# A new opening for an attention and mixture-of-experts kernel: loads in head order, three banks for the running sum, first passes before the bias rows

## The chip, the cores and the metric

The kernel runs on one core of a Trainium2 chip. The metric is the device time of one execution in microseconds (us); lower is better. TensorE (PE) multiplies, ACT (ScalarE), DVE (VectorE) and POOL (GpSimd) do the element-wise work, and SP (SyncE) issues most of the DMAs. PEld is TensorE's loading of weights, which overlaps its matmuls.

## The reference

Attention with a bias that forgets, then a routed layer of experts. There are 8 batches, 8 heads, 576 positions and a head size of 64.

```
scores = q @ k.T / sqrt(64)                       # per batch and head
cum    = cumsum(maximum(s, 0), axis=-1)
scores = where(causal, -1e9, scores + minimum(-(cum[:, None] - cum[None, :]), 0))
attn   = softmax(scores)
x      = attn @ v                                 # to (8 * 576, 512)
logits = x @ w_gate + modality_bias[modality_id]  # 8 experts
e      = argmax(logits); gate = softmax(logits)[e]
out    = gate * (relu(x @ w1[e]) @ w2[e])
```

## The kernel before

The class `Attn` works on 32 pairs, each of two batches (`ab` = 0, 1) of one head. A pair has nine chunks of scores in the order `ORDER = (3, 7, 2, 6, 8, 1, 5, 0, 4)`: chunks 0 to 3 are four blocks of 128 queries of the first batch, 4 to 7 those of the second, and chunk 8 is the last 64 queries of both. A chunk's scores come from two passes of TensorE into one PSUM bank. The first pass (L307, L321 for chunk 8) multiplies QH by KA, that is, the high half of q by the high half of k on partitions 0 to 127, with the low half of k on the lower partitions. The second (L308, L322) multiplies QL by KB: 64 partitions hold the low half of q and the high half of k, and 12 more hold the bias. Of these, ten rows of QL are constant ones and zeros (`rows`), ten rows of KB are taken from `ek`, and two rows of QL are the queries' own sums (`eq`) against rows of -1 in KB. `ek` holds the running sum less its value at the start of each block, in a high half (lower 64 partitions) and a low half (upper 64).

DVE evicts a chunk with the causal mask `mk` and the row's extreme (L310, L324), ACT takes the exponential (L330), TensorE transposes it (L340), ACT or DVE copies it into PT (L343, L359), and TensorE multiplies by V (L380) and by `pw` and `pq` (L274), which hold the identity and the gate's weights. There are four banks for scores (`sp`, SPB = 4). From one pair to the next GpSimd prepares QH, QL and KA (`prep`: L250 makes high halves, L254 low halves), and SP places rows of `ek` and `eq` (`place`: L207, L209). Loads of q, k and v stand in `load_qk` and `load_v` (L232, L237), with two buffers for q and k and three for v.

The order of the instructions on each engine is fixed ahead of the run by a scheduler that goes by program order and readiness; `issue_after` puts an instruction behind another one on the same engine. Each engine takes its instructions in that order and waits at the one whose inputs are missing.

The opening is the constructor. It loads s (576 columns, 128 partitions), pairs 0 and 1 of q, k and v, and the gate's weights (`setup`). ACT scales s by 8 (L84); DVE forms the running sum with three scans into two banks (L92); ACT copies its upper half (L99) and makes `ek`'s parts (L108); DVE makes the low half (L109). ACT also makes the unit of `pq` (L141), QL's constant rows of both buffers (L180, L181), `eq` (L119, L121), and pair 0's part of KB (L192). GpSimd makes masks (L167 to L174) and pair 0's QH and KA (L196 to L198), DVE pair 0's QL (L193). `prep(1)` on GpSimd and the hook `R.consts` at step 7 (L514 to L536) follow during pair 0.

Of the kernel before, what the change touches and what calls it, by code (L numbers as in the profile page):

```python
# [7 lines left out]
F32 = mybir.dt.float32  # L8
F32R = mybir.dt.float32r
# [22 lines left out]

class Attn:
# [3 lines left out]
    def __init__(self, ctx, tc, qkv, s, ident, wg):  # L37
# [9 lines left out]
        self.xo = self.ps2.tile([P, 512], F32, name="ox")  # L47
        self.QH = [c.tile([P, 2, 640], F32R, name=f"QH{u}") for u in range(2)]
        self.QL = [c.tile([P, 2, 640], F32R, name=f"QL{u}") for u in range(2)]
# [22 lines left out]
        eq = self.eq = t1.tile([P, KW], F32R, name="eq")  # L72
# [6 lines left out]
        nc.vector.memset(self.pw, 0.0)  # L79
        self.unit(self.pq, 0)  # L80
        self.setup(wg)
        s8 = t1.tile([P, KW], F32, name="s8")
        for k in (slice(0, 256), slice(256, KW)):
            i = nc.scalar.activation(s8[:, k], sr[:, k], AF.Relu, scale=8.0)  # L84
        with self.tc.issue_after(i.ins):
            self.rows(ho, 0)
        cum = [self.ps1.tile([P, 512], F32, name="sp", bufs=SPB) for _ in range(2)]
        last = 0.0
        for c, k in ((cum[0], slice(0, 256)), (cum[0], slice(256, 512)), (cum[1], slice(0, 64))):
            w = k.stop - k.start  # L90
            at = 512 if c is cum[1] else k.start
            nc.vector.tensor_tensor_scan(c[:, k], s8[:, at:at + w], zz.broadcast_to([P, w]), last, ALU.add, ALU.add)  # L92
            last = c[:, k.stop - 1:k.stop]
        nb = t1.tile([P, 5], F32, name="nb")
        nc.vector.tensor_scalar(nb[:, :4], cum[0][:, 0:512:P], -1.0, None, ALU.mult)
        nc.vector.tensor_scalar(nb[:, 4:], cum[1][:, :1], -1.0, None, ALU.mult)
        cl = self.ps1.tile([P, 512], F32, name="pt")
        with self.tc.issue_after(self.act):
            i = nc.scalar.copy(cl[up], cum[0][up])  # L99
        self.act = i.ins  # L100
        ekf = ek.bitcast(F32)
        for c in (3, 2, 1, 4, 0):
            n = min(P * (c + 1), KW)
            with self.tc.issue_after(self.act):
                for g in range(2 if c == 4 else 1):
                    k = slice(512 * g, min(n, 512 * g + 512))
                    w = k.stop - k.start
                    i = nc.scalar.activation(ek[:, c, k], cum[g][:, :w], AF.Identity, bias=nb[:, c:c + 1])  # L108
                    lo = nc.vector.scalar_tensor_tensor(ek[up, c, k], (cum[1] if g else cl)[up, :w], nb[up, c:c + 1], ekf[up, c, k], ALU.add, ALU.subtract)  # L109
            self.act = i.ins  # L110
        self.prep0(raw, 0)

        dg = ekf.rearrange("p c k -> p (c k)")
        up = slice(64, P)

        def own(u, ab):
            with self.tc.issue_after(self.act):
                r = slice(64 * u + 32 * ab, 64 * u + 32 * ab + 32)
                nc.scalar.copy(eq[r, 64 * ab:64 * ab + 512].rearrange("p (c q) -> p c q", c=4),  # L119
                               dg[r, :2816].rearrange("p (c x) -> p c x", c=4)[:, :, :P])  # L120
                self.act = nc.scalar.copy(eq[r, 512 * (1 - ab):512 * (1 - ab) + 64], dg[r, 2816:]).ins  # L121

        own(0, 0)
        own(0, 1)
        self.hold[0] = lo.ins
        for ab in range(2):
            own(1, ab)
            with self.tc.issue_after(self.act), self.tc.issue_after(self.hold[0]):
                self.prep0(raw, 1 + ab)
        self.place(0)  # L130
        with self.tc.issue_after(self.act):
            self.rows(ho, 1)
        with self.tc.issue_after(self.act):
            self.unit(self.pw, XW)
        self.place(1)

    def unit(self, t, w):

        for ab in range(2):
            rows = slice(64 * ab, 64 * ab + 64)  # L140
            self.act = self.nc.scalar.copy(t[rows, :, w * ab:w * ab + 64], self.ident[rows, 64 * ab:64 * ab + 64].unsqueeze(1).broadcast_to([64, 8, 64])).ins  # L141

    def save(self, u):
# [7 lines left out]
        nc.sync.dma_start(self.eqd[:, u], self.eq.bitcast(F32)[r])  # L151

    def hot(self, t1):
# [14 lines left out]
        nc.gpsimd.affine_select(out=self.mk[:, 384:512], in_=self.mk[:, 384:512], pattern=[[-1, P]],  # L168
                                compare_op=ALU.is_ge, fill=NEG, base=0, channel_multiplier=1)
        nc.gpsimd.memset(self.KB[1].bitcast(F32)[64:96], -1.0)  # L170
        for ab in range(2):
            rows = slice(64 * ab, 64 * ab + 64)
            nc.gpsimd.affine_select(out=self.mk[rows, 736:], in_=self.mk[rows, 736:], pattern=[[-1, 64]],
                                    compare_op=ALU.is_ge, fill=NEG, base=0, channel_multiplier=1)  # L174
        return ho

    def rows(self, ho, u):
        nc = self.nc
        for a, (m, l) in enumerate(((0, 512), (64, 0))):
            nc.scalar.copy(self.QL[u][64:96, a, m:m + 512].rearrange("p (c q) -> p c q", c=4), ho[64:96, :4].unsqueeze(2).broadcast_to([32, 4, P]))  # L180
            self.act = nc.scalar.copy(self.QL[u][64:96, a, l:l + 64], ho[64:96, 4:5].broadcast_to([32, 64])).ins  # L181

    def prep0(self, raw, part):
# [6 lines left out]
        if part:  # L190
            for a in (part - 1,):
                self.act = nc.scalar.copy(KB[lo, a], rk[lo, a]).ins  # L192
                self.hold[0] = nc.vector.tensor_tensor(QL[lo, a, :KW], rq[lo, a], QHf[lo, a, :KW], ALU.subtract).ins  # L193
            return
        for a in range(2):
            nc.gpsimd.tensor_scalar(QH[:, a, :KW], rq[:, a], 1.0, 1.0, ALU.mult, ALU.mult)  # L196
            nc.gpsimd.tensor_scalar(KA[:, a], rk[:, a], 1.0, 1.0, ALU.mult, ALU.mult)
            self.last = nc.gpsimd.tensor_tensor(KA[lo, a], rk[lo, a], KAf[lo, a], ALU.subtract).ins  # L198

    def place(self, pi):  # L200
# [3 lines left out]
        if pi < 8:  # L204
            for u, ab in ((0, 0), (0, 1), (1, 0), (1, 1)):
                r = 32 * ab + pi
                nc.sync.dma_start(KB[64 + 5 * u:69 + 5 * u, ab], self.ek.bitcast(F32)[64 * u + r:64 * u + r + 1])  # L207
                if u:
                    self.sp = nc.sync.dma_start(QL[74:76, ab, :KW], self.eq.bitcast(F32).rearrange("(u p) k -> u p k", u=2)[:, r]).ins  # L209
# [1077 lines left out]
```

## Time and profile before

| what | value |
|---|---|
| median of three runs | 848.71 us (848.46 to 849.37) |
| the profiled execution | 848.76 us |
| its span in the profile | 847.0 us, 16786 instructions |
| TensorE busy | 809.5 us, 96% of the span |
| weight loads | 702.4 us, 83% |
| DVE, ACT, GpSimd busy | 554.7, 537.7 and 359.3 us (65%, 63%, 42%) |
| DMA | 182.01 MB, mean 215 GB/s |

The span is the time from the first to the last recorded work of the execution; its own time has a little around it. Busy shares are means over stages with different limits. All times below are microseconds from the start of the span.

### The profile page before, as it was taken

What the parts mean: (1) busy time and instruction counts of PE and PEld (TensorE: products, weight loads), DVE (VectorE), ACT (ScalarE), POOL (GpSimd) and SP (SyncE); (2) the same over time, 40 slices, a digit from 0 to 9 for tenths busy, and PEclk for the clock granted to TensorE, in tenths of its full rate; (3) what the DMA queues carried; (4) which work ended last, traced back from release to release, by engine and by line L of the source; (5) the groups of instructions that cost most, each with busy time, mean ns of one, the idle gap of its engine ahead of it and who ended that gap; (6) DMA issues with size and microseconds to landing.
All of it is one profiled execution on the core that took longest, in us unless ns stands there. A gap on an engine that the chain in (4) does not pass through costs nothing. (4 is left out here: it accounts for less than half of the span.)

```text
span 847.0 us, 16786 instructions
## 1 busy us (share of the span) xinstructions
PE 809.5 (96%) x5636; PEld 702.4 (83%) x5636; DVE 554.7 (65%) x1516; ACT 537.7 (63%) x1287; POOL 359.3 (42%) x379
## 2 busy tenths in 40 slices
PE   3999999999999999999999999999999999999993
PEld 2888888888888887887888999998888899999872
DVE  6666667666766667666579876555666666565772
ACT  7888888788888888876365454444445555454561
POOL 9668767888679876992400010000000000000000
PEclk9999999999999999999999999999999999999997
DMA  5675555776557655547598776655555666655950
GB/s 180 191 219 176 176 176 177 225 226 205 167 154 233 194 176 175 188 159 280 187 382 303 287 273 252 223 206 209 207 200 216 249 252 252 250 224 208 336 196 7
DMA packets 69336, 182.01 MB, mean 215 GB/s; under 512 B 9727, under 2 KB 9727, under 8 KB 69120
## 3 DMA queue, kind: packets, MB, share of 16 engines
q1 hardware_dynamic: 63408, 160.86, 56.1%
q0 software_dynamic: 5840, 20.06, 6.1%
q8 instruction: 45, 0.74, 0.3%
q14 instruction: 43, 0.35, 0.1%
HBM read 144.76 MB, written 26.80 MB: 203 GB/s over the span
## 5 line engine op out<-in xcount | busy, mean ns | idle before, releaser
L977 POOL DMA_INDIRECT out<-ys,oi x36 | 36.2, 1006 | 369.7 <-DVE ys L976 262.6
L310 DVE CUSTOM_DVE_ANT_0 pe<-sp,mk 128x512 f32<-128x512 f32 (+3 forms) x256 | 120.6, 488 | 57.2 <-PE sp L308 53.3
L330 ACT ACTIVATE pe<-pe,mx 128x512 f32<-128x512 f32 (+3 forms) x256 | 145.1, 567 | 14.1 <-DVE mx L310 8.3
L993 ACT ACTIVATE hT<-hp 128x512 fp32r<-128x512 f32 x72 | 42.8, 596 | 166.6 <-PE hp L991 147.9
L343 ACT COPY PT<-pt 128x512 f32<-128x512 f32 (+3 forms) x256 | 107.3, 419 | 31.3 <-PE pt L340 27.4
L340 PE MATMUL pt<-ident,pe 128*128 128x128 f32 x640 | 120.3, 283 | 0.4 <-ACT PT L343 0.2
L380 PE MATMUL o<-PT,V 128*64 128x320 f32 (+4 forms) x896 | 106.9, 364 | 6.1 <-DVE PT L359 6.1
L307 PE MATMUL sp<-KA,QH 128*128 128x256 f32 (+2 forms) x256 | 99.8, 399 | 11.7 <-POOL KA L198 11.5
L380 PEld LDWEIGHTS o<-PT,V 128*64 128x64 f32 x896 | 70.2, 136 | 43.0 <-DVE PT L359 13.0
L991 PE MATMUL hp<-xT,wcb 128*128 128x256 f32 x648 | 89.7, 282 | 1.1 <-DVE hT L994 1.1
L340 PEld LDWEIGHTS pt<-ident,pe 128*128 128x128 f32 x640 | 76.0, 144 | 16.7 <-ACT PT L343 7.4
L308 PE MATMUL sp<-KB,QL 76*128 76x256 f32 (+2 forms) x256 | 87.0, 342 | 2.6 <-DMA QL<-eq 2.5
L991 PE MATMUL hp<-xT,wca 128*128 128x256 f32 x624 | 87.3, 282 | 0.7 <-ACT xT L947 0.5
L254 POOL TENSOR_TENSOR KA<-rawk,KA 64x576 fp32r<-64x576 f32 x62 | 87.0, 1422 | 0.2
L254 POOL TENSOR_TENSOR QL<-rawq,QH 64x576 fp32r<-64x576 f32 x62 | 86.5, 1412 | 0.1
L994 DVE SCALAR_TENSOR_TENSOR hT<-hp,hT 128x512 fp32r<-128x512 f32 x72 | 49.5, 688 | 55.4 <-ACT hT L993 55.4
L991 PEld LDWEIGHTS hp<-xT,wcb 128*128 128x128 f32 x648 | 83.1, 188 | 2.0 <-DVE hT L994 1.3
L991 PEld LDWEIGHTS hp<-xT,wca 128*128 128x128 f32 x624 | 80.4, 188 | 1.8 <-issue 1.0
L970 PE MATMUL y<-wcb,hT 128*128 128x512 f32 x336 | 81.2, 398 | 0.0
L970 PEld LDWEIGHTS y<-wcb,hT 128*128 128x128 f32 x336 | 62.7, 188 | 14.6
L250 POOL TENSOR_SCALAR KA<-rawk 128x576 fp32r<-128x576 f32 x62 | 41.9, 688 | 65.5 <-PE sp L307 47.7
L991 PE MATMUL hp<-xT,wcc 128*128 128x256 f32 x456 | 64.7, 281 | 0.5 <-DVE hT L994 0.5
(280 smaller groups left out, 1627.4 us busy)
## 6 DMA issues: line engine op xcount, KB each, us to landing
wrbw<-in_w SPq DMA_DIRECT2D x104, 512.0 KB
wraw<-in_w SPq DMA_DIRECT2D x56, 512.0 KB
rawq<-in_qkv SPq DMA_DIRECT2D x32, 576.0 KB
rawk<-in_qkv SPq DMA_DIRECT2D x32, 576.0 KB
xg<-lists SPq DMA_DIRECT2D x18, 576.0 KB
V<-in_qkv SPq DMA_DIRECT2D x32, 320.0 KB
KB<-KA SPq DMA_DIRECT2D x62, 144.0 KB
lists<-z SPq DMA_DIRECT2D x8, 576.0 KB
```

Of the source, the lines that this page charges most:

```text
L254: self.last = nc.gpsimd.tensor_tensor(o, i, h, ALU.subtract).ins
L307: self.pe.append(nc.tensor.matmul(sp[:, :nn], QH[:, q0:q0 + P], KA[:, ab, :nn], start=True, stop=False).ins)
L308: self.pe.append(nc.tensor.matmul(sp[:, :nn], QL[:EXT, q0:q0 + P], KB[:EXT, ab, :nn], start=False, stop=True).ins)
L310: ins = nc.vector.tensor_tensor_reduce(out=t[:, :n], in0=sp[:, :n], in1=self.mk[:, 512 - n:512], scale=-0.125, scalar=3.0e38, op0=ALU.add, ...
L330: self.act = nc.scalar.activation(t[:, :n], t[:, :n], AF.Exp, bias=m, scale=-1.0, accum_out=st["sums"][:, o:o + 1]).ins
L340: self.pe.append(nc.tensor.transpose(out=pt[:, P * j:P * j + P], in_=pe[:, P * j:P * j + P], identity=self.ident).ins)
L343: cp(w[:, :, v:v + P], pt[:, :P * (c + 1)].rearrange("p (j q) -> p j q", q=P))
L380: m = nc.tensor.matmul(o[r, f - q0:q1 - q0], V[:, ab, j, :], PT[ab][:, PTS * j + f if j < 4 else PTW - 64:PTS * j + q1 if j < 4 else PTW], ...
L970: self.last[0] = nc.tensor.matmul(y[u], hT[:, a, f, P * u:P * u + P], W[4 + f // 2][:, c, 512 * (f % 2):512 * (f % 2) + 512], start=f == 0 ...
L991: nc.tensor.matmul(hp[:, u], W[k][:, a, f:f + P], xT[:, c, k], start=k == 0 and i == 0, stop=k == 3 and i == 2)
L993: hi = nc.scalar.activation(hs, hp, AF.Relu)
L994: lo = nc.vector.scalar_tensor_tensor(hT[:, 1, 2 * m:2 * m + 2], hp, 0.0, hs.bitcast(F32), ALU.max, ALU.subtract)
```

## The change

- **Loads.** s comes in two halves, pair 0's q and k in four loads, one batch at a time, and pair 1's k ahead of its q. V[1] and pair 2's q and k are issued at the end of the constructor, behind pair 1's rows, in place of pair 2's load at step 7 of pair 0.
- **Running sum.** Three banks of 256, 256 and 64 columns; the last value goes through a small SBUF tile; `ek` is made in pieces of at most 256 columns.
- **Bias rows.** `eq` is gone: its two rows go from `ek` into QL by DMA (`place_q`, two for the blocks and two for the last 64 queries). KB's ten rows of one batch go in one DMA (`place_k`), the first of them issued by ACT. `save` copies own rows out of `ek` in four DMAs. QL's constant rows are made once, half by ACT and half by GpSimd, and copied to the second buffer by DMA; QL lies in a longer tile.
- **Pair 0 and pair 1.** The part of KB that holds k comes by DMA from KA in place of ACT copies. Pair 1's high halves are made by ACT (`prep1`) in place of GpSimd; its low halves stay in `prep`.
- **GpSimd.** The masks go behind pair 0's KA; the units of `pw` and `pq` are made by GpSimd at step 6. `R.consts` goes to step 14.
- **TensorE.** Forty transposes of the identity into a scratch bank at the start, and the first passes of chunks 3, 7, 2 and 6 of pair 0 ahead of any second pass, with four such transposes behind each. The second passes of pair 0 keep the order of the chunks until the first product with V.

```diff
-        self.xo = self.ps2.tile([P, 512], F32, name="ox")
+        self.QLx = [c.tile([P, 1408], F32R, name=f"QL{u}") for u in range(2)]
...
-        nc.sync.dma_start(sr, s)
-        raw = self.load_qk(0)
-        self.raw[1] = self.load_qk(1)
-        for pi in range(2):
-            self.V[pi] = self.load_v(pi)
+        for k in HALVES:
+            nc.sync.dma_start(sr[:, k], s[:, k])
+        raw = self.raws()
+        for a in range(2):
+            for u in range(2):
+                nc.sync.dma_start(raw[u][:, a], self.qkv[0, :, KW * (2 * u + a):KW * (2 * u + a + 1)])
+        nc.vector.memset(self.pw, 0.0)
+        self.raw[1] = self.load_qk(1, (1, 0))
+        self.setup(wg)
+        self.V[0] = self.load_v(0)
...
+        self.warm(WARM)
+        self.rows(ho)
...
+        cum = [self.ps1.tile([P, 512], F32, name="sp", bufs=SPB) for _ in range(3)]
+        for g, w in enumerate((256, 256, 64)):
+            nc.vector.tensor_tensor_scan(cum[g][:, :w], s8[:, 256 * g:256 * g + w], zz.broadcast_to([P, w]), last, ALU.add, ALU.add)
+            n = (w + P - 1) // P
+            nc.vector.tensor_scalar(nb[:, 2 * g:2 * g + n], cum[g][:, 0:w:P], -1.0, None, ALU.mult)
+            if g < 2:
+                last = end[:, g:g + 1]
+                nc.vector.tensor_copy(last, cum[g][:, w - 1:w])
+                with self.tc.issue_after(self.act):
+                    self.act = nc.scalar.copy(cl[up, 256 * g:256 * g + w], cum[g][up, :w]).ins
...
+        self.place_k(0, 0)
+        self.sp = nc.sync.dma_start(self.QL[1].bitcast(F32)[64:74, :, :KW], self.QL[0].bitcast(F32)[64:74, :, :KW]).ins
+        self.place(0)
+        for ab in range(2):
+            with self.tc.issue_after(self.hold[0]):
+                self.prep0(raw, 1 + ab)
+        with self.tc.issue_after(self.act):
+            self.prep1()
+        with self.tc.issue_after(self.last):
+            self.masks()
+        with self.tc.issue_after(self.sp):
+            self.sp = nc.sync.dma_start(self.KB[1].bitcast(F32)[:64], self.KA[1].bitcast(F32)[64:]).ins
+        with self.tc.issue_after(self.sp):
+            self.place(1)
+        with self.tc.issue_after(self.sp):
+            self.raw[2] = self.load_qk(2)
+        with self.tc.issue_after(self.sp):
+            self.V[1] = self.load_v(1)
+        self.more = {6: self.units}
...
+    def prep1(self):
+        rq, rk = self.raw[1]
+        for t, r in ((self.KA[1], rk), (self.QH[1], rq)):
+            for a in range(2):
+                self.act = nc.scalar.copy(t[:, a, :KW], r[:, a]).ins
...
+            self.last = self.nc.gpsimd.tensor_copy(t[rows, :, w * ab:w * ab + 64], self.ident[rows, 64 * ab:64 * ab + 64].unsqueeze(1).broadcast_to([64, 8, 64])).ins
...
         for a in range(2):
             nc.gpsimd.tensor_scalar(QH[:, a, :KW], rq[:, a], 1.0, 1.0, ALU.mult, ALU.mult)
             nc.gpsimd.tensor_scalar(KA[:, a], rk[:, a], 1.0, 1.0, ALU.mult, ALU.mult)
+            nc.sync.dma_start(KB.bitcast(F32)[lo, a], KAf[up, a])
...
+    def warm(self, n):
+        for _ in range(n):
+            i = self.nc.tensor.transpose(out=self.xo[:, :P], in_=self.ident, identity=self.ident).ins
+        return i
...
+            if st["pi"] == 0 and not st["s"]:
+                for j in ORDER[:SPB]:
+                    self.high(st, j)
+                    with self.tc.issue_after(self.pe[-1]):
+                        self.pe.append(self.warm(WARM2))
+            sp = st["high"][i] if i in st["high"] else self.high(st, i)
...
-                with self.behind():
+                with self.behind() if pi or not self.pe else self.tc.issue_after(self.pe[-1]):
...
-                if k % 9 == 7 and pi + 2 < npair:
+                if k % 9 == 7 and 0 < pi < npair - 2:
...
-            setup = {5: A.consts, 7: R.consts, 17: lambda: A.save(0), 26: lambda: A.save(1), 20: lambda: R.setup(mid, mb, A.t1p)}
+            setup = {**A.more, 5: A.consts, 14: R.consts, 17: lambda: A.save(0), 26: lambda: A.save(1), 20: lambda: R.setup(mid, mb, A.t1p)}
```

## Rows read from the trace of the kernel before

**Rows 1.** Windows: busy of PE, PEld, DVE, ACT, POOL; granted clock; DMA share; GB/s.

```profile
0.00:20.00 20.00, 5.55 (x14) 3.66 (x15) 12.54 (x31) 15.73 (x35) 18.03 (x29) 1.00 0.58 190
20.00:847.00 827.00, 804.00 (x5623) 698.78 (x5622) 542.18 (x1488) 521.99 (x1253) 341.28 (x351) 0.99 0.63 215
...
5.00:10.00 5.00, 0.00 (x0) 0.00 (x0) 3.13 (x8) 4.99 (x14) 3.87 (x6) 1.00 1.00 378
```

**Rows 2.** Waits, 0 to 25 us: waiter and releaser, total, times, longest.

```profile
PE sp L307 <- POOL KA L198: 11.5, 2, 10.2
...
PE sp L308 <- DMA QL<-eq: 2.5, 1, 2.5
```

**Rows 3.** Timeline of ACT and DVE: start, length, engine, line, work, idle before.

```profile
3.59 0.78 ACT L84 ACTIVATE s<-sr 128x256 f32<-128x256 f32 x2 [1.53 <-DMA sr<-in_s]
...
4.04 0.70 DVE L92 TENSOR_TENSOR_SCAN sp<-s,zz 128x256 f32<-128x256 f32 x1 [0.20 <-ACT s L84]
...
6.73 0.57 ACT L99 COPY pt<-sp 64x512 f32<-64x512 f32 x1
...
8.04 2.37 DVE L109 SCALAR_TENSOR_TENSOR ek<-pt,nb,ek 64x512 fp32r<-64x512 f32 x4 [1.83 <-ACT ek L108]
...
10.51 0.38 DVE L109 SCALAR_TENSOR_TENSOR ek<-pt,nb,ek 64x128 fp32r<-64x128 f32 x1
...
10.92 3.08 DVE L193 TENSOR_TENSOR QL<-rawq,QH 64x576 fp32r<-64x576 f32 x2
```

**Rows 4.** Timeline of SP's DMA issues: start, length of the issue.

```profile
9.73 2.03 SPq L237 DMA_DIRECT2D V<-in_qkv  x1
...
11.88 2.40 SPq L207 DMA_DIRECT2D KB<-ek  x3
...
14.38 0.57 SPq L209 DMA_DIRECT2D QL<-eq  x1
```

**Rows 5.** Timeline of TensorE, pair 0 and the start of pair 1.

```profile
16.21 1.08 PE L308 MATMUL sp<-KB,QL 76*128 76x512 f32 x2 [2.47 <-DMA QL<-eq]
...
17.77 0.61 PE L321 MATMUL sp<-KA,QH 128*128 128x288 f32 x1 [0.47 <-DVE mx L310]
...
18.92 1.05 PE L340 MATMUL pt<-ident,pe 128*128 128x128 f32 x4
...
20.25 0.44 PE L322 MATMUL sp<-KB,QL 76*128 76x288 f32 x1
...
20.49 0.44 PE L321 MATMUL sp<-KA,QH 128*128 128x288 f32 x1
...
21.41 0.60 PE L340 MATMUL pt<-ident,pe 128*128 128x128 f32 x4
...
23.07 0.47 PE L307 MATMUL sp<-KA,QH 128*128 128x512 f32 x1
...
28.88 0.65 PE L274 MATMUL ox<-pw,oT 128*128 128x144 f32 x4
```

**Rows 6.** Timeline of DVE's evictions and ACT's exponential of chunk 8.

```profile
17.01 0.69 DVE L310 CUSTOM_DVE_ANT_0 pe<-sp,mk 128x512 f32<-128x512 f32 x1 [3.02 <-PE sp L308]
...
18.84 0.69 DVE L310 CUSTOM_DVE_ANT_0 pe<-sp,mk 128x512 f32<-128x512 f32 x1 [1.13 <-PE sp L308]
...
22.18 0.78 ACT L330 ACTIVATE pep<-pep,mx 128x576 f32<-128x576 f32 x1
```

**Rows 7.** Timeline of GpSimd, and last its low halves by line (ns, least, median, most).

```profile
4.77 0.86 POOL L173 TENSOR_SCALAR_AFFINE_SELECT mk<-mk 64x64 f32<-64x64 f32 x2
...
5.72 0.75 POOL L196 TENSOR_SCALAR QH<-rawq 128x576 fp32r<-128x576 f32 x1
...
7.47 0.67 POOL L197 TENSOR_SCALAR KA<-rawk 128x576 fp32r<-128x576 f32 x1 [1.00 <-DMA rawk<-in_qkv]
...
12.22 2.31 POOL L250 TENSOR_SCALAR KA<-rawk 128x576 fp32r<-128x576 f32 x2
...
L254 POOL TENSOR_TENSOR KA<-rawk,KA x62: 1400/1420/1447, 18.5 to 366.6; 64x576 fp32r<-64x576 f32 x62
```

More of the change, by code (lines that the diff above doesn't have):

```diff
@@ L30 @@
 QUIET = (1, 5, 6)
+HALVES = slice(0, 256), slice(256, KW)
+WARM = 40
+WARM2 = 4
 class Attn:
@@ L78, in __init__ @@
             nc.vector.memset(ek.bitcast(F32)[:, c, P * (c + 1):], 0.0)
-        nc.vector.memset(self.pw, 0.0)
-        self.unit(self.pq, 0)
-        self.setup(wg)
+        self.xo = self.ps2.tile([P, 512], F32, name="ox")
+        self.warm(WARM)
+        self.rows(ho)
         s8 = t1.tile([P, KW], F32, name="s8")
[L83 to L96, printed above, removed]
-        cl = self.ps1.tile([P, 512], F32, name="pt")
-        with self.tc.issue_after(self.act):
-            i = nc.scalar.copy(cl[up], cum[0][up])
-        self.act = i.ins
+        for k in HALVES:
+            with self.tc.issue_after(self.act):
+                self.act = nc.scalar.activation(s8[:, k], sr[:, k], AF.Relu, scale=8.0).ins
+        cum = [self.ps1.tile([P, 512], F32, name="sp", bufs=SPB) for _ in range(3)]
+        cl = self.ps1.tile([P, 512], F32, name="pt")
+        nb, last = t1.tile([P, 5], F32, name="nb"), 0.0
+        end = t1.tile([P, 2], F32, name="end")
+        for g, w in enumerate((256, 256, 64)):
[7 more added lines that the diff above has]
+                    self.act = nc.scalar.copy(cl[up, 256 * g:256 * g + w], cum[g][up, :w]).ins
         ekf = ek.bitcast(F32)
@@ L103, in __init__ @@
             n = min(P * (c + 1), KW)
-            with self.tc.issue_after(self.act):
-                for g in range(2 if c == 4 else 1):
-                    k = slice(512 * g, min(n, 512 * g + 512))
+            for g in range((n + 255) // 256):
+                k = slice(256 * g, min(n, 256 * g + 256))
+                with self.tc.issue_after(self.act):
+                    self.act = nc.scalar.activation(ek[:, c, k], cum[g][:, :k.stop - k.start], AF.Identity, bias=nb[:, c:c + 1]).ins
+            for t, k in ((cl, slice(0, min(n, 512))), (cum[2], slice(512, n))):
+                if k.start < k.stop:
@@ new lines, in __init__, with masks @@
+        self.more = {6: self.units}
+    def masks(self):
+        nc = self.nc
+        nc.gpsimd.affine_select(out=self.mk[:, 384:512], in_=self.mk[:, 384:512], pattern=[[-1, P]],
+                                compare_op=ALU.is_ge, fill=NEG, base=0, channel_multiplier=1)
+        for ab in range(2):
+            rows = slice(64 * ab, 64 * ab + 64)
+            nc.gpsimd.affine_select(out=self.mk[rows, 736:], in_=self.mk[rows, 736:], pattern=[[-1, 64]],
+                                    compare_op=ALU.is_ge, fill=NEG, base=0, channel_multiplier=1)
+        self.last = nc.gpsimd.memset(self.KB[1].bitcast(F32)[64:96], -1.0).ins
@@ L204, in place @@
         if pi < 8:
[L205 to L209, printed above, removed]
+            for ab in range(2):
+                if pi or ab:
+                    self.place_k(pi, ab)
+                self.place_q(pi, ab)
+            for ab in range(2):
+                self.place_q(pi, 2 + ab)
         else:
@@ L226, in consts, with raws, load_qk @@
             nc.vector.memset(t[64:, PTW - 64:], 0.0)
-    def load_qk(self, pi):
+    def raws(self):
+        return [self.ld.tile([P, 2, KW], F32, name="rawq"), self.ld.tile([P, 2, KW], F32, name="rawk")]
+    def load_qk(self, pi, order=(0, 1)):
         nc = self.nc
-        raw = [self.ld.tile([P, 2, KW], F32, name="rawq"), self.ld.tile([P, 2, KW], F32, name="rawk")]
-        for u in range(2):
-            nc.sync.dma_start(raw[u], self.qkv[pi, :, 2 * KW * u:2 * KW * u + 2 * KW].rearrange("p (a k) -> p a k", a=2))
+        raw = self.raws()
+        for u in order:
+            self.sp = nc.sync.dma_start(raw[u], self.qkv[pi, :, 2 * KW * u:2 * KW * u + 2 * KW].rearrange("p (a k) -> p a k", a=2)).ins
         return raw
@@ L256, in prep @@
         lo, up = slice(0, 64), slice(64, P)
-        for a in range(2):
+        for a in range(2 if pi > 1 else 0):
             high(KA[:, a], rk[:, a])
-        for a in range(2):
+        for a in range(2 if pi > 1 else 0):
             nc.sync.dma_start(KB.bitcast(F32)[lo, a], KAf[up, a])
         yield
-        for a in range(2):
+        for a in range(2 if pi > 1 else 0):
             high(QH[:, a, :KW], rq[:, a])
@@ L292, in start, with high @@
         return st
+    def high(self, st, i):
+        ab, c = i // 4, i % 4
+        nn, q0, u = max(P * (c + 1), 256), 704 * ab + P * c, st["pi"] % 2
+        sp = st["high"][i] = self.ps1.tile([P, 512], F32, name="sp", bufs=SPB)
+        QH = self.QH[u].rearrange("p a x -> p (a x)")
+        self.pe.append(self.nc.tensor.matmul(sp[:, :nn], QH[:, q0:q0 + P], self.KA[u][:, ab, :nn], start=True, stop=False).ins)
+        return sp
     def score(self, st, i):
```

82 lines of the change are left out of this document (43 added, 39 removed).

## The prediction

> **What bounds the kernel now.** I read the windows first. In the first 20 us TensorE does 5.55 us of work, in the 827 us after that 804.0, which is 97% [rows 1]. So the body is bound by TensorE and the opening by something else: a microsecond saved in the opening should shift the whole body by a microsecond, and one saved on ACT, DVE or GpSimd later should not show.
>
> The waits of the first 25 us name what TensorE stands behind: twice GpSimd's preparation of KA (L198), then a DMA into QL [rows 2]. The timeline gives the chain that ends in that DMA. The two scalings of s start at 3.59 and the scans at 4.04, but ACT reaches its copy of the sum only at 6.73, since pq's unit and QL's rows stand before it; the low rows of ek on DVE start at 8.04 and end at 10.51 + 0.38 = 10.89 [rows 3]. SP is still issuing V until 9.73 + 2.03 = 11.76, so the first KB row leaves at 11.88, and the first QL row, which waits for ACT's copies into eq, at 14.38 [rows 4]. The second pass of chunk 3 starts at 16.21, 1.83 us after that issue began and 1.26 us after it ended. In TensorE's order a pass of chunk 8, for which a bank must come free, stands at 17.77 ahead of chunk 7's second pass [rows 5]. The milestones of the opening are the evictions of chunk 3 (17.01) and chunk 7 (18.84) and the exponential of chunk 8 (22.18) [rows 6].
>
> The granted clock reads 1.00 [rows 1], but the passes tell its level: at 20.25 and 20.49 passes of 288 columns follow each other in 0.24 us, which is 1.2 GHz. Four transposes take 1.05 us at 18.92 and 0.60 us at 21.41, so by then the level is the upper one. TensorE had worked almost without a gap since 17.77 [rows 5].
>
> **The running sum and ek.** s arrives in halves, so the first scaling starts no later than 3.59. pq's unit and half of QL's rows leave ACT. The scans of 256 columns keep their 0.70; one-column copies of the last sum come between them. Those have no row: nothing if hidden, at most a whole scan step of 0.70 if they break the flow; being one column wide they are nearest to nothing, and I take 0.15 each, and as much for nb. The second scan ends at 4.04 + 0.70 + 0.15 + 0.15 + 0.70 = 5.75. ACT then copies its half (between half of 0.57 and 0.57, taken 0.36) until 6.1, and makes chunk 3's two halves of ek (0.39 each, half of the scalings' 0.78), until 6.9. The other pieces, four more of 256 columns and three shorter ones, of 0.25 or so, end at about 9.2. DVE's low rows took 10.89 - 8.04 = 2.85 in all [rows 3]; from 7.0 they could end at 9.85, but chunk 4's wait for ACT, and I take 10.2 for the whole of ek, 0.7 earlier.
>
> **Own rows and the queues.** eq and its eight ACT copies go, and so does the wait for them. After ek, ACT issues the first KB row itself; SP's three took 2.40, 0.80 each, and a QL row 0.57, so the bounds are 0.57 to 0.80; I take 0.7, until 10.9. SP issues five more (0.57, 0.72, and three of 0.57) from 10.2 to 13.2 [rows 4]. With the 1.26 us from above, chunk 3's rows land at 12.0 and 12.2, chunk 7's at 13.35, chunk 8's last at 14.5. The copy of QL's rows into the second buffer stands ahead of them; it does not need ek, so it costs nothing if SP is idle before 10.2. V[1] is deferred, so SP should be through sooner than 11.76; if it is not, these landings move by up to 1.6 us.
>
> **GpSimd.** QH and KA now come in four loads of one head each, in the order needed. KA's first half ends the same number of bytes that came first before; GpSimd took those by 5.72 and waited until 7.47 for the next tile [rows 7]. These are the bounds; I take 5.72, because the bytes are the same. From 7.47 its five steps took until 12.22, 4.75 us, so KA of the second head is ready at 10.5. The masks (0.86 for two of the three) and a memset go behind it, some 2.2 us, to 12.7; chunk 3's eviction wants the first by 13.9. GpSimd's half of QL's rows lies before the load, in the room that the masks leave. The four ACT copies for pair 1, 0.67 each by GpSimd's row of the same shape, run from 10.9 to 13.6, before the first exponential at 14.7: hidden, but a load late by over 1.1 us would hold up every exponential.
>
> QL's two low halves took 3.08 us on DVE [rows 3], with GpSimd working beside them. The Trainium skill (SBUF — State Buffer, Who interferes with whom) says that a VectorE instruction with two SBUF inputs and a GpSimd instruction that reads SBUF shut each other out for their whole length; a step of 576 columns in twice the time of a 512-column copy (0.57) agrees with it. By that rule the halves, with GpSimd partly in masks, would need about 1.4 us and end at 11.6; by their old length they end at 13.3. Either lies before chunk 7's row at 13.35, so the sum does not hang on it.
>
> **TensorE.** Forty transposes of the identity start at about 2.1, when the identity is there. At 0.15 each (0.60 for four) they end at 8.1, at 0.26 (1.05 for four) at 12.6 [rows 5]. I take the middle, 10.35. Four first passes (0.25 each at most) with four transposes (0.6) behind each make 13.65. With the forty done in time, KA at 10.5 sets the second of the four, and they end at 12.95. I take 13.3 for chunk 3's second pass, against 16.21. Chunk 7's is next in the new order, and its row is there at 13.35. Eviction came 0.80 after the pass; at the upper level I take 0.6: chunk 3 at 13.9, then 0.69 + 0.08 later chunk 7 at 14.65. ACT's exponential of chunk 3 starts at 14.7; two of 512 columns (0.73), two of 384 (0.6) and a copy (0.57) put chunk 8's at 18.0.
>
> **The sum.** Milestones before and after: 17.01 to 13.9, 18.84 to 14.65, 22.18 to 18.0, which is -3.1, -4.2, -4.2 [rows 6]. From there TensorE is full, as it was: -4.2 us. Does pair 1 follow? It began at 23.07 [rows 5], so at 18.9 now. GpSimd's four low halves (1.42 each) follow QH at 13.6 and end at 15.0, 16.4, 17.8 and 19.2; the first head's KA is there at 17.8, in time. Then GpSimd makes the units. It has no row for this: four steps of 0.67, as one input of 576 columns, or of 1.42, as two, so 2.7 to 5.7; one input is nearer. They end at about 22.2, or 25.2; the gate's matmul wants pw at 28.88 - 4.2 = 24.7 [rows 5, 7]. Hidden, or at worst 0.5 late. Pair 2's loads move ahead, which relieves GpSimd and not TensorE. The three DMAs more in each save (0.57 to 0.80 each) delay only SP's rows for a later pair.
>
> The profiled execution took 848.76 us, 847.0 of it the span; the median of the runs is 848.71. 848.71 - 4.2 gives 844.5.
>
> **Rivals.**
> (a) The gain is larger. Chunk 3 comes at 12.95, and TensorE also wins back the half that it lost at the lower level from 17.77 to 21.3: 4.2 + 0.35 + 1.75 gives 842.4. Against it: DVE and ACT set the pace of the first chunks, not TensorE.
> (b) SP is not free at 10.2, since V's issue took 2.03 us while the DMA engines were full [rows 1, 4]. Chunk 7's and 8's rows come 1.6 later and so do the evictions: 846.1.
> (c) The loads don't move, and the pairs wait for them. DMA is full between 5 and 10 us at 378 GB/s [rows 1]. Pair 1's k was there by 12.22 [rows 7]; if with the new order its q came 5 us after that, ACT's copies would stand before the exponentials and nothing would be left: 848.5.
> (d) Slower: the warm-up itself is the bound. If all 56 transposes take 0.26 and the four passes 0.45, chunk 3's second pass comes at 2.1 + 14.6 + 1.8 = 18.5; nothing else is waited for then, and chunk 8's exponential comes 4.9 later at 23.4, 1.2 more than before, and a little more as the low level goes on: 850.3. It decides from the point where a transpose takes about 0.24 on average. For it: TensorE ran at the lower level up to 21 us. Against it: it rose after steady work, and the transposes are that. The Trainium skill (TensorE: Matmul & The Clock Gate, Part 1) has it that the array starts at half rate and that activity releases it; the rows agree.
>
> **How the numbers follow.** Forecast 0.50 (843.5 to 845.6), (a) 0.15, (b) 0.16, (c) 0.12, (d) 0.07. 0.2% is 1.7 us, about what a measurement of this kernel can tell from no change: faster 0.81, same 0.12, slower 0.07. The range takes in the forecast, (a) and (b), and reaches the edge of (c): 841.8 to 848.0.
>
> **What would show it.** Right: ek's last low rows near 10.2 with SP's first row right behind; four transposes in 0.6 us by 11; chunk 3's second pass near 13.3, chunk 7's eviction near 14.65; pair 1's first pass near 18.9, and the later pairs as much earlier. Wrong: TensorE waiting for KA past 11, ACT waiting for rawq, GpSimd still in the units when the gate's matmul is due, or pairs that follow each other more slowly than before.

## The result and the profile after

The change made the kernel slower: 851.46 us (849.90 to 854.63, 11 runs) against 848.52 us (847.67 to 849.66, 11 runs) before, a ratio of 1.0041 with a 95% interval of [1.0033, 1.0050]. The forecast was 844.5. The profiled execution took 854.63 us, its span 852.9; it is the longest of the 11, so the stalls below, read from its trace, come to more (5.9 us against the span of before) than the medians differ (2.9).

One milestone per pair places the time: the start of the twenty products with V on TensorE, read from its timeline.

| start, us | pair 0 | pair 1 | pair 2 | pair 3 | pair 4 | pair 10 | span |
|---|---|---|---|---|---|---|---|
| before | 25.7 | 37.0 | 48.6 | 60.3 | 71.7 | 140.7 | 847.0 |
| after | 26.3 | 41.8 | 55.1 | 66.5 | 77.7 | 146.6 | 852.9 |

So 0.6 us is lost in pair 0, 4.2 more by pair 1 and 1.6 more by pair 2, of which some 0.6 comes back; 5.9 stands at pair 10 and at the end. The opening, where all of the gain was to come from, gave nothing, and a stall that the prediction didn't look for came behind it.

The timeline of the opening after: GpSimd, ACT, DVE and TensorE (start, length, engine, line, work, idle before).

```profile
5.58 0.68 POOL L224 TENSOR_SCALAR QH<-rawq 128x576 fp32r<-128x576 f32 x1 [3.36 <-DMA rawq<-in_qkv]
6.21 0.19 POOL L191 TENSOR_SCALAR_AFFINE_SELECT ho<-ho 128x5 f32<-128x5 f32 x1
...
6.43 0.76 ACT L210 CAST QL<-ho 10x512 fp32r<-10x512 f32 x2 [4.37 <-POOL ho L191]
7.22 0.78 ACT L94 ACTIVATE s<-sr 128x256 f32<-128x256 f32 x2
...
7.67 1.09 DVE L101 TENSOR_TENSOR_SCAN sp<-s,zz 128x256 f32<-128x256 f32 x1 [3.85 <-ACT s L94]
...
2.12 5.89 PE L247 MATMUL ox<-ident 128*128 128x128 f32 x40 [2.12 <-POOL ident masks.py:199]
11.97 0.79 PE L369 MATMUL sp<-KA,QH 128*128 128x512 f32 x1 [3.96 <-POOL KA L227]
...
17.74 1.41 PE L391 MATMUL sp<-KB,QL 76*128 76x512 f32 x4
...
18.68 0.69 DVE L393 CUSTOM_DVE_ANT_0 pe<-sp,mk 128x512 f32<-128x512 f32 x1 [2.60 <-PE sp L391]
...
22.72 0.78 ACT L413 ACTIVATE pep<-pep,mx 128x576 f32<-128x576 f32 x1
```

Read it from the releasers in brackets. GpSimd's fixed order has QH, which waits for q, ahead of the second select of `ho`, a step of 0.19 us; ACT's copy of `ho` into QL waits 4.37 us for that select, the scalings of s stand behind the copy, and the scan starts at 7.67 where it started at 4.04 [rows 3]. TensorE does its forty transposes and then has nothing until 11.97, because GpSimd makes KA as late. Against [rows 6], chunk 3's eviction comes at 18.68 (17.01) and chunk 8's exponential at 22.72 (22.18).

SP's issues, to hold against [rows 4]:

```profile
9.14 2.38 SPq L306 DMA_DIRECT2D V<-in_qkv  x1
11.62 1.46 SPq L226 DMA_DIRECT2D KB<-KA  x2
13.17 1.01 SPq L124 DMA_DIRECT2D QL<-QL  x1
14.65 0.60 SPq L277 DMA_DIRECT2D QL<-ek  x1
```

The first own row leaves SP at 14.65; `ek` is done at about 14.6, so here both are late together. TensorE's clock in the windows (columns as in [rows 1]):

```profile
2.10:4.70 2.60, 2.58 (x12) 2.58 (x13) 1.66 (x10) 0.00 (x0) 0.12 (x1) 1.00 0.94 266
...
12.00:16.00 4.00, 3.52 (x12) 2.69 (x13) 3.95 (x8) 1.82 (x7) 3.63 (x6) 0.50 0.62 168
16.00:18.00 2.00, 2.00 (x11) 1.93 (x10) 0.08 (x1) 1.87 (x4) 0.00 (x0) 0.50 0.07 25
...
42.00:44.00 2.00, 2.00 (x9) 1.26 (x10) 0.92 (x5) 1.31 (x4) 2.00 (x6) 0.60 0.90 194
```

The forty transposes in two parts, 2.0 to 4.7 us and from 5.2 us on:

```profile
2.12 2.82 PE L247 MATMUL ox<-ident 128*128 128x128 f32 x12 [2.12 <-POOL ident masks.py:199]
...
5.01 3.00 PE L247 MATMUL ox<-ident 128*128 128x128 f32 x26
```

The first twelve take 2.82 us, or 0.24 each; the last 26 take 3.00, or 0.12 each. So they begin at the lower level and come to the upper one near 5 us. The granted clock reads 1.00 in the first part all the same (the window from 2.10), as it did in the kernel before over passes at the lower level [rows 1].

After 3.96 us without work the granted clock is 0.50, the lower level, from 12 to 18 us: what the transposes had brought up was down again when the scores came. The Trainium skill (TensorE: Matmul & The Clock Gate, Part 1) has it that an idle array goes back to half rate; the trace agrees.

The stall at pair 1, DVE, GpSimd and TensorE in the timeline:

```profile
36.60 1.15 DVE L605 TENSOR_SCALAR ecap<-e 128x8 f32<-128x8 f32 x1 [0.54 <-ACT e L603]
37.66 2.91 DVE L607 TENSOR_SCALAR ew<-e 128x8 f32<-128x8 f32 x1
...
36.31 1.40 POOL L323 TENSOR_TENSOR KA<-rawk,KA 64x576 fp32r<-64x576 f32 x1
37.68 0.29 POOL L611 TENSOR_SCALAR_AFFINE_SELECT tri<-tri 128x128 bf16<-128x128 bf16 x1
37.94 1.30 POOL L319 TENSOR_SCALAR KA<-rawk 128x576 fp32r<-128x576 f32 x2
39.21 1.30 POOL L319 TENSOR_SCALAR QH<-rawq 128x576 fp32r<-128x576 f32 x2
...
41.83 4.29 PE L463 MATMUL o<-PT,V 128*64 128x320 f32 x20 [3.34 <-DVE PT L442]
```

The same two steps in the kernel before, at step 7:

```profile
26.41 0.17 DVE L522 TENSOR_SCALAR ecap<-e 128x8 f32<-128x8 f32 x1
26.49 0.16 DVE L524 TENSOR_SCALAR ew<-e 128x8 f32<-128x8 f32 x1
```

Two steps of eight columns in `R.consts`, now at step 14, take 1.15 and 2.91 us on DVE. At step 7 they took 0.17 and 0.16, while GpSimd idled. Here GpSimd works without a gap through both: `ecap` ends at 37.75, where GpSimd's low half ends (37.71), and `ew` at 40.57, just behind QH (40.51). DVE's copies of PT stand behind it, TensorE waits 3.34 us for them, and falls to the lower level (0.60 in the window from 42), so that the products take 4.29 us, where others take 2.6. The Trainium skill (SBUF — State Buffer, Who interferes with whom) says that a tensor_scalar on VectorE in its two-port mode and GpSimd lock each other out, the later one for the whole instruction of the other. The trace agrees with a lock, but `ew` waited through several instructions and not one; in which mode the steps ran it doesn't show.

### The profile page after: what moved, and what is told of

It reads as the page before. It is cut to its first block, busy times and chain, and to the rows that moved or that the text cites. A ratio compares the mean times of both kernels' runs of the same rounds, so it can differ in the third digit from the quotient of the medians.

```text
span 852.9 us, 16898 instructions
## 1 busy us (share of the span) xinstructions
PE 818.9 (96%) x5692; PEld 710.9 (83%) x5692; DVE 558.4 (65%) x1519; ACT 531.7 (62%) x1275; POOL 359.0 (42%) x381
## 5 line engine op out<-in xcount | busy, mean ns | idle before, releaser
L1060 POOL DMA_INDIRECT out<-ys,oi x36 | 36.3, 1010 | 369.7 <-DVE ys L1059 263.5
L463 PE MATMUL o<-PT,V 128*64 128x320 f32 (+4 forms) x896 | 108.9, 368 | 9.3 <-DVE PT L442 9.3
L1053 PEld LDWEIGHTS y<-wcb,hT 128*128 128x128 f32 x336 | 62.7, 188 | 14.6
L319 POOL TENSOR_SCALAR KA<-rawk 128x576 fp32r<-128x576 f32 x60 | 39.6, 673 | 67.1 <-PE sp L369 61.7
```

The lines of the kernel that those rows point to most:

```text
L463: m = nc.tensor.matmul(o[r, f - q0:q1 - q0], V[:, ab, j, :], PT[ab][:, PTS * j + f if j < 4 else PTW - 64:PTS * j + q1 if j < 4 else PTW], ...
L1053: self.last[0] = nc.tensor.matmul(y[u], hT[:, a, f, P * u:P * u + P], W[4 + f // 2][:, c, 512 * (f % 2):512 * (f % 2) + 512], start=f == 0 ...
```

## The experiments

Each kernel is the one after with the edits named, unless said otherwise. Ratios are to the kernel before, timed on the same chip. Its own medians in these timings lie between 847.38 and 848.57 us, so across timings the differences to it are compared, and a few tenths of a microsecond between two versions say nothing. Places of products come from one profiled execution each.

**The constants on GpSimd (e2)** take the two steps away from DVE:

```diff
-        nc.vector.tensor_scalar(self.ecap, self.e, float(CAP), None, ALU.mult)
+        nc.gpsimd.tensor_scalar(self.ecap, self.e, float(CAP), None, ALU.mult)
...
-        nc.vector.tensor_scalar(self.ew, self.e, -1.0, 8.0, ALU.mult, ALU.add)
+        nc.gpsimd.tensor_scalar(self.ew, self.e, -1.0, 8.0, ALU.mult, ALU.add)
```

> The changed kernel with two constants (ecap and ew, 8 columns each) made by GpSimd in place of DVE, still at step 14. Theory (in the changed kernel DVE's two tiny steps stood 1.15 and 2.91 us behind GpSimd's back-to-back work, TensorE then waited 3.3 us for PT and fell to its lower level): the two steps vanish from DVE, the product with V starts about 3.7 us sooner and takes 2.6 in place of 4.3 us, so 4 to 5 us less than the changed kernel, about 846.5. Rival (the stall of pair 1 comes from loads, SP's longer saves or the pairs' order): within 1 us of the changed kernel, 850.5 or more.

Measured: 849.65 us (848.71 to 850.46), ratio 1.0010 [1.0000, 1.0019]. On GpSimd the steps take 0.24 and 0.20:

```profile
38.04 0.24 POOL L605 TENSOR_SCALAR ecap<-e 128x8 f32<-128x8 f32 x1
38.35 0.20 POOL L607 TENSOR_SCALAR ew<-e 128x8 f32<-128x8 f32 x1
```

The products of pairs 0 and 1 start at 27.1 and 38.7, 11.6 apart (15.5 in the kernel after, 11.3 before), and those of pair 1 take 2.54. The stall is gone, as the theory had it, but the time lies between its 846.5 and the rival's 850.5: the difference to before falls from 2.9 us to 1.3. Pair 0's products, which the edit doesn't touch, are 0.8 later than in the profile after; the granted clock is 0.50 here from 20 to 24 us.

**The constants at step 14 in the kernel before (b1)**, that move alone:

```diff
-            setup = {5: A.consts, 7: R.consts, 17: lambda: A.save(0), 26: lambda: A.save(1), 20: lambda: R.setup(mid, mb, A.t1p)}
+            setup = {5: A.consts, 14: R.consts, 17: lambda: A.save(0), 26: lambda: A.save(1), 20: lambda: R.setup(mid, mb, A.t1p)}
```

> The kernel before with one line of the change: the hook of the constants at step 14 in place of step 7. Theory (what costs is that DVE's two tiny steps fall into a stretch in which GpSimd works without a pause): DVE's ecap or ew takes over 1 us in place of 0.17, TensorE waits as long, 2 to 5 us slower than before, 850.5 to 853.5. Rival (the stall needs the rest of the change): 848.5.

Measured: 853.72 us (851.55 to 854.92), ratio 1.0060 [1.0037, 1.0082]; products at 25.8, 40.1 (4.3 long) and 53.3. One number in one line costs 5.4 us (four runs). Its stall has two parts:

```profile
PE o L380 <- DVE PT L359: 1.4, 1, 1.4
...
PE pt L353 <- ACT PT L343: 1.1, 1, 1.1
ACT tok L517 <- POOL ti L516: 1.0, 1, 1.0
```

These are waits from 34 to 41 us. DVE's `ecap` takes 1.38 us and `ew` 0.73; ahead of them ACT waits in its order for GpSimd's iotas, and its copies of PT wait behind.

**GpSimd's order (e3)**: pair 0's QH behind GpSimd's rows of QL, so that `ho` comes first; **both (e4)** is this with the edit of e2.

```diff
-        self.prep0(raw, 0)
+        with self.tc.issue_after(self.last):
+            self.prep0(raw, 0)
...
-                    nc.gpsimd.tensor_scalar(o, i, 1.0, 1.0, ALU.mult, ALU.mult)
+                    self.last = nc.gpsimd.tensor_scalar(o, i, 1.0, 1.0, ALU.mult, ALU.mult).ins
```

> The changed kernel with pair 0's QH and KA on GpSimd put behind the one-hot tile and QL's rows, so that ho does not stand behind a wait for the load of q. Theory (this order held up ACT's scaling by 3.6 us): the scaling of s starts at about 3.6 in place of 7.2, the exponential of chunk 8 comes about 3 us sooner (19.5 in place of 22.7), and the kernel 3 us sooner than the changed one, 848.5, if DVE's two tiny steps of step 14 still stall. Rival (the loads or the warm transposes set the opening anyway): exponential of chunk 8 within 1 us of 22.7, time 850.5 or more.

Measured: 851.39 us (848.88 to 853.61), ratio 1.0029 [1.0015, 1.0044]; products at 26.1, 38.2 and 49.9. The scalings start at 3.29, but chunk 8's exponential only at 22.16, 0.6 sooner and not 3, so the rival's figures came. In this profile `ecap` took 1.07 us and `ew` 0.16: how long they are locked out differs between these profiles.

> Both edits together: the two constants by GpSimd and the new GpSimd order. If the two losses are separate they add: about 7 to 8 us less than the changed kernel, 843.5 to 844.5, faster than before by 0.5%. Rival (each edit only uncovers the next wait): 846 to 848.5, no or hardly any gain on before.

Measured: 850.41 us (849.37 to 852.25), ratio 1.0025 [1.0016, 1.0035], above the figures of the theory and of the rival. The scalings start at 3.29 and `ek` ends at 10.50, close to the 10.2 of the prediction, and yet the second pass starts only 0.8 us sooner:

```profile
8.82 2.83 SPq L307 DMA_DIRECT2D V<-in_qkv  x1
11.75 1.16 SPq L227 DMA_DIRECT2D KB<-KA  x2
13.01 1.01 SPq L125 DMA_DIRECT2D QL<-QL  x1
14.12 0.70 SPq L278 DMA_DIRECT2D QL<-ek  x1
...
16.94 1.42 PE L392 MATMUL sp<-KB,QL 76*128 76x512 f32 x4 [3.48 <-DMA QL<-ek]
```

Now SP's queue holds it: the rows are ready at 10.5 and the first on that queue leaves at 14.12. TensorE idles 3.48 us, the granted clock is 0.50 in the window from 20 to 24 us, and pair 0's products start at 27.1.

**A bridge of transposes (e8)**: e4 with ten transposes, not four, behind each first pass.

```diff
-WARM2 = 4
+WARM2 = 10
```

> Both edits with SP's order as in the changed kernel, but ten transposes in place of four behind each of the four first passes, so that TensorE works through the wait for the rows until about 16.9. Theory (the fall to the lower level after the idle stretch costs pair 0 about half of its 7 us there): second pass still near 17, pair 0's product with V at 23.5 to 24.5 in place of 27.1, 2.5 to 3.5 us faster than both edits alone, 847 to 848. Rival (the level costs little since DVE and ACT set the pace): within 1 us of both edits alone, 849.5 or more.

Measured: 849.35 us (848.71 to 850.62), ratio 1.0009 [0.9999, 1.0018], 1.1 under e4, short of the theory's 2.5 to 3.5. The clock still falls, but less (0.91 and 0.67 from 16 to 20 and from 20 to 24 us, against 0.81 and 0.50). Pair 0's products start at 26.8, only 0.3 sooner than in e4 and not at 23.5 to 24.5, and pairs 1 to 3 start within 0.1 us of e4's. So the 1.1 us is not shown to come from the bridge.

**SP's order (e5)**: e4 with the gate weights and V[0] behind pair 0's own rows.

```diff
-        self.setup(wg)
-        self.V[0] = self.load_v(0)
...
         self.place(0)
+        with self.tc.issue_after(self.sp):
+            self.setup(wg)
+        with self.tc.issue_after(self.sp):
+            self.V[0] = self.load_v(0)
```

> Both edits (constants by GpSimd, GpSimd order), and on SP the gate's weights and V[0] behind pair 0's rows in place of ahead of them. Theory (with ek ready at 10.5 the wait has moved to SP, which issues the gate's weights and V until 11.65 and then three copies before the first own row at 14.12; TensorE idles from 13.5 to 16.9 and falls to its lower level until 25): the first own row leaves SP at about 10.7, chunk 3's second pass comes at about 13.5 in place of 16.9, no stretch at the lower level after it, pair 0's product with V starts at 21 to 22 in place of 27.1, and the kernel takes 844 to 845.5. Rival (the rows' landing is held by the loads in the queues, not by SP's order): second pass at 16 or later, 849 to 850.5.

Measured: 851.81 us (850.99 to 854.21), ratio 1.0040 [1.0025, 1.0055], above the figures of the theory and of the rival. The opening is the predicted one:

```profile
10.52 0.64 SPq L280 DMA_DIRECT2D QL<-ek  x1
...
13.19 1.35 PE L394 MATMUL sp<-KB,QL 76*128 76x512 f32 x4
...
21.54 0.34 SPq L304 DMA_DIRECT2D rawq<-in_qkv  x1
...
21.95 2.27 PE L466 MATMUL o<-PT,V 128*64 128x320 f32 x19
...
28.00 1.31 POOL L322 TENSOR_SCALAR KA<-rawk 128x576 fp32r<-128x576 f32 x2 [5.61 <-DMA rawk<-in_qkv]
```

The second pass is at 13.19 (predicted 13.3), the eviction at 13.81 (13.9), chunk 8's exponential at 17.85 (18.0); pair 0's products start 3.7 us sooner than before. But pair 1's start at 38.5, 1.5 later than before. The last row and the waits from 30 to 40 us tell why:

```profile
ACT tok L603 <- POOL ti L602: 4.4, 1, 4.4
...
PE sp L372 <- POOL KA L326: 2.9, 1, 2.9
```

Pair 2's loads, issued at 21.54 and 21.91, land at 28.0 and GpSimd idles 5.61 us for them; the iotas of the constants then stand between its two halves of KA, and ACT waits 4.4 us in its order for the iotas. A shorter opening reaches pair 2 before pair 2 is there. In the kernel before, the same chain just met TensorE:

```profile
22.14 0.54 SPq L232 DMA_DIRECT2D rawq<-in_qkv  x1
...
28.46 1.31 POOL L250 TENSOR_SCALAR KA<-rawk 128x576 fp32r<-128x576 f32 x2 [4.08 <-DMA rawk<-in_qkv]
...
33.77 2.80 POOL L254 TENSOR_TENSOR KA<-rawk,KA 64x576 fp32r<-64x576 f32 x2
...
35.65 0.40 PE L307 MATMUL sp<-KA,QH 128*128 128x512 f32 x1
```

Pair 2's loads were issued at 22.14 there. The change, which meant to move them ahead, issues them at 21.94 (21.54 in e5), behind pair 1's rows, so they land hardly sooner.

**No transposes (e6: none of the 56; e7: none of the 16 between the first passes)**, from e5:

> The same as the run with SP's new order but without any of the 56 transposes. Theory that the transposes pay: chunk 3's second pass 0.5 to 1 us sooner, but the chunks of pair 0 at the lower level for 3 us or more, so 1 to 2 us slower than with them. Rival (DVE and ACT set the pace of pair 0's first chunks): within 0.5 us of the run with them, or faster by up to 1 us.

> SP's new order with the 40 transposes at the start but without the 16 between the first passes. If the 16 only delay the second passes: 0.5 to 1 us faster than with them. If they keep TensorE at its upper level over the wait for the rows: 1 to 3 us slower.

Measured: e6 850.59 us (849.66 to 851.80), ratio 1.0023 [1.0013, 1.0032]; e7 850.21 us (847.82 to 852.69), ratio 1.0025 [1.0015, 1.0035]. Pair 0's products start at 23.3 and 23.4, 1.3 and 1.5 later than in e5, and yet the medians are 1.2 and 1.6 lower, with intervals that overlap e5's: where pair 2 sets the time, a faster pair 0 is worth nothing. Why they are lower is not shown.

**All constants on GpSimd behind pair 2's halves (e9)**, and with that **pair 2's loads ahead of V[0] and the gate weights (e10)**. e9 is e5 with the two casts of `R.consts` on GpSimd too and the call at step 15; e10 moves `self.raw[2] = self.load_qk(2)` up to right behind `place(0)`, and V[0] ahead of the weights.

> This is the kernel after with GpSimd's order mended, pair 0's first own row ahead of V[0] and the gate weights on SP's queue, and the constants of rows (casts, powers, products) all on GpSimd, behind the halves of pair 2's KA. Theory that pair 2's loads are the next bound (issued about 21.5 to 22 us, landed 28.0, and GpSimd takes KA of pair 2 only from there): pair 0's V product at about 21.9, pair 1's at 35.5 to 36.5, the time 847 to 848. Rival that only the constants held pair 1: its V product at 33 to 34, the time 844.5 to 845.5.

Measured: 849.74 us (849.43 to 850.39), ratio 1.0027 [1.0016, 1.0038]; products at 22.7, 37.5 and 49.5. Pair 1 and the time are later than either theory's figures; the constants alone were not the hold.

> As the last one, with pair 2's loads of q and k put on SP's queue right behind the first own rows of pair 0, ahead of V[0] and the gate weights. Theory that these loads are the next bound: V products of pairs 0, 1 and 2 at about 21.9, 33.3 and 44.7 us, the time 844.5 to 845.5, some 3.5 us under before. Rival that pair 1's own rows, which now stand behind the loads, come late: pair 1's V product at 35.5 or later, the time 847.5 or more.

Measured: 847.98 us (846.39 to 850.07), ratio 1.0003 [0.9995, 1.0012]: 1.8 under e9, so the loads did hold part of it, and not under before, as the rival had it. Products at 24.4, 37.4 and 48.6, those of pair 3 at 60.2: against e9 nothing is gained at pair 1, 0.9 at pair 2 and 2.2 at pair 3. Pair 1's own rows come late behind the gate weights, whose issues take until 18.11:

```profile
PEld sp L393 <- DMA KB<-KA: 2.1, 1, 2.1
PE sp L393 <- DMA QL<-ek: 1.9, 1, 1.9
```

**e10 without any transposes (e11)**:

> As the last one, without any of the 56 transposes of the opening. Theory that they pay by the higher level of TensorE's clock in pair 0's scores: V product of pair 0 at about 23.3 us, the time 1 to 2 us above the last one's. Rival that they don't: within 0.5 us.

Measured: 849.61 us (847.73 to 852.42), ratio 1.0026 [1.0012, 1.0039], 1.6 above e10, the theory's time. Its milestones don't bear the theory out: the products start at 24.4, 36.3 and 48.5, no later than e10's, and the loss of the profile, itself 2.5 above the median, stands at pair 3 (64.0 against 60.2): TensorE waits 3.2 us there for GpSimd's KA, and GpSimd 7.4 us before it, which the profile puts down to the second save's copies (`eqd<-ek`). What the transposes are worth is not settled by it.

**Gate weights behind pair 1's rows (e12)**: e10 with `self.setup(wg)` behind `place(1)`.

> As the kernel with pair 2's loads ahead, with the four gate-weight loads (issued from 15.21 to 18.11 us there, ahead of KB<-KA and the own rows of pair 1) put behind the last own row of pair 1. Theory that SP's order holds pair 1: own rows of pair 1 issued 2.5 to 3 us earlier, the second pass of its chunk 3 at 21.0 to 22.0 in place of 23.70, V products of pairs 0 and 1 at about 22 and 34.5, the time 845 to 846. Rival that GpSimd's share of pair 1's halves (last one ends at 20.1) and DMA landing hold it: second pass still at 23 or later, the time 847.5 to 848.5.

Measured: 849.22 us (847.09 to 852.16), ratio 1.0016 [1.0003, 1.0028]. Products at 22.8, 34.5, 47.5 and 61.6: pairs 0 and 1 as its theory has it, 2.9 and 2.5 us ahead of before, and all of it given back by pair 3. The time is above both theories' figures.

```profile
31.23 0.39 SPq L303 DMA_DIRECT2D rawq<-in_qkv  x1
31.68 0.42 SPq L303 DMA_DIRECT2D rawk<-in_qkv  x1
32.15 0.48 SPq L181 DMA_DIRECT2D ekd<-ek  x1
32.67 5.18 SPq L185 DMA_DIRECT2D eqd<-ek  x4
...
46.10 0.50 PE L371 MATMUL sp<-KA,QH 128*128 128x512 f32 x1 [1.74 <-POOL KA L325]
```

GpSimd starts on pair 3's k at 38.89, 7.2 us after its issue; right behind the loads stands the save, 720 KB more for the same DMA engines (busy share 1.02 at 297 GB/s from 32 to 36 us; without it, in e13, 0.93 at 362). The save's four small copies also hold SP for 5.18 us, so that pair 2's own rows leave at 37.95.

**Saves later (e13)**, from e12, and the same edit on e4 (**e14**):

```diff
-            setup = {... 17: lambda: A.save(0), 26: lambda: A.save(1), ...}
+            setup = {... 40: lambda: A.save(0), 49: lambda: A.save(1), ...}
```

> As the kernel with the gate weights late, with the two saves (steps 17 and 26: one copy of 720 KB and four small ones each, on SP's queue right behind the loads of pairs 3 and 4) put at steps 40 and 49. Theory that these copies share the DMA engines with the loads and so give back what the opening gained (V products of pairs 0 to 4 there at 22.8, 34.5, 47.5, 61.6 and 74, of before at 25.7, 37.0, 49, 60.3 and 71.7): V products at 22.8, 34.5, 46, 57.5 and 69, the time 844.5 to 846. Rival that the loads come late by themselves (two buffers of raw, issue behind the place of the pair before): V products of pairs 2 and 3 still at 47 and 60 or later, the time 848 or more.

Measured: 847.36 us (847.05 to 849.17), ratio 0.9987 [0.9978, 0.9996], the one version that beats the kernel before, by 1.1 us. Products at 23.7, 35.4, 46.5, 58.1 and 69.3 (pair 10 at 139.4, 1.3 ahead of before; the span is 845.6, 1.4 less). GpSimd has pair 3's k 5.6 us after its issue:

```profile
36.94 1.32 POOL L321 TENSOR_SCALAR KA<-rawk 128x576 fp32r<-128x576 f32 x2 [2.56 <-issue]
```

The places of pairs 2 and 3 are near those of its theory, the time is 1.4 above the figure's upper end: of the 2.4 us gained at pair 4, 1.1 goes again by pair 10. TensorE waits once there, 0.8 us between 84 and 100 us, again for GpSimd's KA; in the kernel before it doesn't. The edit takes two things away at once, the save's bytes behind the loads and its hold on SP (pair 2's rows leave at 33.31 in place of 37.95, pair 4's q at 40.43 in place of 45.19); which of them weighs more no run separates.

> The kernel after with the powers on GpSimd and GpSimd's order mended (850.41 us, 2.1 above before, in an earlier run), and the two saves put at steps 40 and 49. Theory that the saves hold pairs 3 and 4: 1 us or more under that run's difference to before. Rival that there, with its later opening, they were covered: no change, 1.5 to 2.5 us above before.

Measured: 851.23 us (849.98 to 854.61), ratio 1.0032 [1.0021, 1.0043] against 1.0025 for e4: no gain, as the rival had it. In e14 the products of pairs 0 to 2 stand at 27.9, 39.4 and 50.8. Its opening came 0.8 later than e4's, and from pair 3 to pair 4 it takes 11.4 us against 11.8, which fits a late opening that hides most of what the saves cost; the two runs are of different timings, and no more is shown.

## Why the prediction was wrong

- **ek.** The prediction let the scaling start "no later than 3.59" and put GpSimd's half of QL's rows "before the load, in the room that the masks leave". The order on GpSimd put `ho` behind the load instead: 7.22, 3.6 us late. With that undone (e4) the step's size was nearly right: 10.50 for 10.2, from a scaling that began 0.3 sooner.
- **Own rows on SP.** "It costs nothing if SP is idle before 10.2": SP was at V until 11.52 and at KB<-KA and QL<-QL until 14.18. This was rival (b) with 1.6 us; e4 against e5 shows 3.6 us at the first QL row (14.12, 10.52) and 3.75 at the second pass (16.94, 13.19). The prediction counted neither the two KB<-KA issues nor the gate weights on that queue.
- **The first passes, evictions and the exponential.** Wrong in the kernel after; right to 0.22 us once order and queue are mended (e5): 13.19, 13.81, 14.43 and 17.85 against 13.3, 13.9, 14.65 and 18.0. Some of that is luck: in e5 the second head's KA was ready at 11.18 (10.5 predicted) and ACT's first row took 1.42 us to issue (0.7), while the forty transposes ended at 9.7 (10.35).
- **QL's two low halves** took 1.42 us in the kernel after and 2.04 in e5, at and above the shorter of the two lengths that the prediction gave (1.4, 3.08). The row given in support of that length was misread: a half took 1.54 in the kernel before, 2.7 times the 0.57 of that copy and not twice, and the copy was ACT's, not DVE's.
- **The transposes** take 5.89 us for the forty, 0.147 on average, about twelve of them at the lower level (in the profile of e4 28 of them, and 7.54 us in all). That is under rival (d)'s 0.24, so it falls. But they end at 8.0, and the idle time behind them takes the level back. What they are worth with the scores in time is 1.3 us at pair 0 (e5, e6); that they pay at the end is not shown (e10, e11).
- **A term that was missing.** `R.consts` at step 14 was not costed. In the profile after it is the largest loss, 4.2 us at pair 1 and 1.7 in the clock behind it; by the medians some 1.6 there (e2), and 5.4 in the kernel before (b1).
- **"From there TensorE is full, as it was": the step that fails even with all that mended.** e5 has -4.3 us at chunk 8's exponential, -3.0 at pair 1's first pass (20.11; 18.9 predicted), -3.7 at pair 0's products and +3.2 at the end. In the kernel before, GpSimd's first half of pair 2's KA ended at 35.2 and the pass that reads it began at 35.65: the pairs followed the opening with 0.45 us to spare. Loads, GpSimd's halves, own rows and saves all have to come sooner before the opening's time counts; e10, e12 and e13 each moved the wait on. "Pair 2's loads move ahead" was a move of 0.2 us. "Three DMAs more in each save (0.57 to 0.80 each) delay only SP's rows" was mis-sized: four of the new copies hold SP for 5.32 us in the kernel after, the one of before 0.70, and the 720 KB beside the loads were left out.

The medians are less well explained than the profiles: e2 takes 1.6 us off the kernel after, e3 next to nothing, and the mended order and constants together (e4) no more than the constants alone. Part of it stands behind the opening: from pair 3 to pair 4 the profiles of e2, e3 and e4 take 12.0, 12.9 and 11.8 us, that of before 11.4. The runs of the kernel after and of e3 spread over 4.7 us, those of before over 2.0; why is open.

## What to carry to other kernels

A gain in an opening is worth no more than the slack of the next stages' preparation: read, for each of the next two or three pairs, when its loads are issued and land and when its last prepared operand is ready, and hold that against the pass that reads it moved forward. A moved call is to be costed with every engine that it touches and with what stands on GpSimd beside it at the new place. And in a static order a step of 0.19 us behind a wait for a DMA costs as much as the wait.

## What the runs showed of the hardware

- An 8-column tensor_scalar on DVE took 0.16 us beside an idle GpSimd and mostly 0.73 to 2.91 us beside a busy one (once 0.16), where it could stay locked out through several of GpSimd's instructions in a row; on GpSimd itself it took 0.20 to 0.24.
- The first KB row cost 1.39 us to issue on ACT in the kernel after (1.42 in e5), the same kind of row 0.50 to 0.58 on SP. V's load issued among the first loads holds SP for 2.0 to 2.9 us, later on mostly for 0.36 to 0.62.
- Six microseconds of transposes brought TensorE to the upper level, from a start at the lower one, but did not hold it there: after 3.5 to 4 us without work in the kernel after and in e4, the granted clock was 0.50 in windows that followed (12 to 18 and 20 to 24 us).
